# A float32 product split into three float32r products, in a fused convolution and feed-forward kernel

## The chip, the cores and the metric

The kernel runs on one core of a Trainium2 chip. The metric is the device time of one execution in microseconds (us). Three executions of the kernel before took 2501.99, 2504.36 and 2504.86 us; the median is 2504.36 us.

## The reference

Eight batches of 3008 positions x 256 channels are convolved along the positions by a filter given in the frequency domain. The result, 24064 tokens of 256 values, goes through a feed-forward layer whose activation is a rational function.

```python
X = np.fft.rfft(x, axis=1)                  # x: (8, 3008, 256), float32
y = np.fft.irfft(X * (filt_r + 1j * filt_i), n=3008, axis=1)
h = y.reshape(24064, 256) @ w_in            # w_in: (256, 2048)
P = a[0] + a[1] * h + a[2] * h**2 + a[3] * h**3
Q = 1.0 + abs(b[0]) * abs(h) + abs(b[1]) * h**2
out = (P / (Q + 1e-06)) @ w_out             # w_out: (2048, 256)
```

## The kernel before

The Fourier transform of length 3008 = 64 x 47 is done as matrix products in three stages. Stage 1 is the transform of length 47 (the matmuls `s`, L435), with sums and differences made by GpSimd beforehand (`fold`, L382). Stage 2 works on 128 rows x 512 columns at a time, twelve pieces `i` for each batch. `product` multiplies the piece by the forward 64-point matrix (`y`, L488: one float32 matmul, which the trace records as two). VectorE multiplies the result by the two filter tiles (L492, L493), and GpSimd makes the complex product of them: `cross` twice (L504, two operations each), then `total` (L510). `halves` splits the sum into two float32r parts, the upper one as a ScalarE copy (L516), the lower one as a GpSimd subtraction (L517). `inverse` multiplies by the inverse 64-point matrix, which is held in two parts as well, with three float32r matmuls (`z`, `product3`, L349), and VectorE copies the result out (L344). Stage 3 (`x`, L572) is the inverse transform of length 47. It gives tokens in chunks of five groups of 94, split into upper and lower parts by ScalarE (L581) and VectorE (L583).

The feed-forward layer runs in 752 units of 512 tokens x 128 hidden values. Each unit has six matmuls in (L606 to L609) and six out (L689 to L691), all float32r, 128 x 512. Between them ScalarE makes five passes, VectorE four (`p` L657, `g_hi` L666, `rest` L674, `g_lo` L680), each with one operand in PSUM, and GpSimd two (`pool_m` L671, `pool_q1` L652). The four passes of VectorE on one unit are spread over several units of program order: `product_out` of unit i - 4 is issued with `product_in` of unit i, after what the convolution puts between. In the last 128 units half of the squares move from ScalarE to GpSimd.

The order of work on TensorE, ScalarE, VectorE and GpSimd is written out by hand. The convolution of the next batch is a generator that the loop over units advances (`pipeline`, L886). Each item that it yields has a cost. A credit grows by 0.6 per unit for batch 1 and by 0.38 for the others, and one item at most is issued per unit. A bare `yield` puts what follows into the next unit:

```python
            if i > 0:
                yield from s.inverse(i - 1)
            if i < 12:
                s.cross(i, 0, 1)
                yield
                s.total(i)
                yield
                s.halves(i)
```

So a step (one y and one z) takes at least four units: y's, z's with the second `cross`, one with `total`, one with `halves`. A stage 3 chunk puts two units of its own in between when its time has come, in all for one chunk in 14 or 15 units. If a chunk needs a batch whose convolution isn't finished, the rest of that batch is issued at once, with no unit between (`run(gen or conv_items(nxt))`, L934).

Batch 0 is done in the head (`head`, L719), where `Plan` (L110) orders the steps by a list of durations and due times and gives each raw weight tile the home that comes free first. Weights 14 and 15 are loaded at unit 0 into fixed homes (`RAW`, L56): 15 into a home of "oe", the tag of the output tiles, of which there are two.

## Time and profile before

| | before |
|---|---|
| median of three executions | 2504.36 us |
| the profiled execution | 2504.63 us |
| its span, first to last instruction | 2502.8 us |
| mean granted share of TensorE's clock | 0.990 |
| TensorE busy | 2451.5 us, 98% |
| VectorE busy | 2279.7 us, 91% |
| ScalarE busy | 2340.8 us, 94% |
| GpSimd busy | 2103.9 us, 84% |

"Busy" is the time in which at least one instruction of the engine runs. Instructions of an engine overlap at their ends, so the time from one start to the next is what an instruction costs its engine, and it is a little shorter than its recorded duration: a 128 x 512 float32r matmul is recorded with 0.39 us, and the next one starts 0.227 us later. The head takes about the first 81 us. The seven further batches run beside the units up to about 2060 us. After that the units run alone.

In the views PE is TensorE, DVE VectorE, ACT ScalarE, POOL GpSimd and SP SyncE, whose queue issues the DMAs. L488 is line 488 of the kernel.

### The profile page before, as it was taken

How to read it: one execution, taken by the hardware profiler on the slowest of the kernel's cores; microseconds unless marked ns; L12 is line 12 of the kernel's file. 1: busy time of each engine (PE TensorE's matmuls, PEld its weight loads, DVE VectorE, ACT ScalarE, POOL GpSimd, SP SyncE). 2: the span in 40 equal slices, each digit the busy share in tenths (PEclk: the TensorE clock that was granted, in tenths of full speed). 3: DMA queues.
4: the chain of work that ended last, by engine and by line, in shares of the span. 5: the costliest groups of instructions: out<-in, count | busy, mean ns of one | idle time of the engine just before them, and what ended most of it. 6: DMA issues, size and time to landing. Idle time of an engine off the chain costs nothing.

```text
span 2502.8 us, 36529 instructions
## 1 busy us (share of the span) xinstructions
PE 2451.5 (98%) x10950; PEld 1958.0 (78%) x10950; DVE 2279.7 (91%) x3554; ACT 2340.8 (94%) x4139; POOL 2103.9 (84%) x2261
## 2 busy tenths in 40 slices
PE   7799989999999999999999999999999999999998
PEld 4578867878787877888788887887788788888887
DVE  7789978999889998999889998899889999999998
ACT  6699979999999999999999999999999999999997
POOL 7788987899868997889868998789868897888887
PEclk9799999999999999999999999999999999999999
DMA  7443242322323232332323322332322210100000
GB/s 264 142 111 89 85 115 77 112 82 84 98 78 100 85 92 78 91 105 84 90 84 90 93 86 77 96 100 84 95 86 81 62 42 17 33 17 17 25 10 19
DMA packets 98727, 205.12 MB, mean 82 GB/s; under 512 B 7967, under 2 KB 54559, under 8 KB 98519
## 3 DMA queue, kind: packets, MB, share of 16 engines
q1 hardware_dynamic: 98519, 202.70, 27.2%
q8 instruction: 88, 1.44, 0.3%
q14 instruction: 120, 0.98, 0.1%
HBM read 130.49 MB, written 72.17 MB: 81 GB/s over the span
## 4 chain that ended last, share of the span: by engine, by line
PE 85%; POOL 6%; DVE 5%; issue 2%; ACT 1%; DMA 1%; SPq 0%; POOLq 0%; DVEq 0%; ACTq 0%
PE o L689 12%; PE o L690 12%; PE o L691 12%; PE h_u L606 12%; PE h_u L607 12%; PE h_u L609 12%; PE x L572 4%; PE s L435 3%; PE y L488 3%; POOL q_u L671 2%; PE z L349 2%; POOL q_u L652 1%; DVE h_u L674 1%; DVE hi_u L666 1%; POOL a_u L640 1%
## 5 line engine op out<-in xcount | busy, mean ns | idle before, releaser
L671 POOL TENSOR_TENSOR q_u<-q_u,hi_u 128x512 f32<-128x512 f32 x752 | 975.3, 1297 | 253.5 <-DVE hi_u L666 231.4
L689 PE MATMUL o<-hi_u,wo_sb 128*128 128x512 f32 x1504 | 660.4, 439 | 0.0
L666 DVE SCALAR_TENSOR_TENSOR hi_u<-h_u,scal,a_u 128x512 fp32r<-128x512 f32 x752 | 557.4, 741 | 51.5 <-ACT a_u L642 44.6
L606 PE MATMUL h_u<-xhl,wi_sb 128*128 128x512 f32 x1504 | 593.5, 395 | 3.9 <-DVE raw L313 3.8
L690 PE MATMUL o<-lo_u,wo_sb 128*128 128x512 f32 x1504 | 588.3, 391 | 7.7 <-DVE lo_u L680 7.7
L691 PE MATMUL o<-hi_u,wo_sb 128*128 128x512 f32 x1504 | 588.5, 391 | 0.0
L607 PE MATMUL h_u<-xhl,wi_sb 128*128 128x512 f32 x1504 | 587.9, 391 | 0.0
L674 DVE SCALAR_TENSOR_TENSOR h_u<-h_u,scal,q_u 128x512 f32<-128x512 f32 x752 | 563.7, 750 | 25.4 <-POOL q_u L671 24.5
L657 DVE SCALAR_TENSOR_TENSOR h_u<-w_u,scal,h_u 128x512 f32<-128x512 f32 x752 | 560.2, 745 | 5.2 <-ACT w_u L621 5.2
L632 ACT ACTIVATE a_u<-q_u,scal 128x512 f32<-128x512 f32 x752 | 549.2, 730 | 0.0
L627 ACT ACTIVATE q_u<-q_u,scal 128x512 f32<-128x512 f32 x752 | 546.8, 727 | 1.9
L652 POOL TENSOR_SCALAR q_u<-q_u,scal 128x512 f32<-128x512 f32 x752 | 526.8, 700 | 1.5 <-ACT a_u L632 1.4
L621 ACT ACTIVATE w_u<-h_u,scal 128x512 f32<-128x512 f32 x752 | 519.6, 691 | 0.0
L614 ACT ACTIVATE q_u<-h_u 128x512 f32<-128x512 f32 x752 | 454.3, 604 | 65.3 <-PE h_u L609 52.2
L680 DVE TENSOR_TENSOR lo_u<-h_u,a_u 128x512 fp32r<-128x512 f32 x752 | 512.5, 682 | 0.1
L609 PE MATMUL h_u<-xhl,wi_sb 128*128 128x512 f32 x1504 | 465.3, 391 | 0.0
L642 ACT ACTIVATE a_u<-a_u 128x512 f32<-128x512 f32 x688 | 438.4, 637 | 0.0
L690 PEld LDWEIGHTS o<-lo_u,wo_sb 128*128 128x128 f32 x1504 | 283.5, 188 | 98.6 <-issue 37.5
L689 PEld LDWEIGHTS o<-hi_u,wo_sb 128*128 128x128 f32 x1504 | 283.3, 188 | 89.2 <-issue 35.7
L606 PEld LDWEIGHTS h_u<-xhl,wi_sb 128*128 128x128 f32 x1504 | 283.7, 189 | 70.0 <-DVE lo_u L680 5.2
L607 PEld LDWEIGHTS h_u<-xhl,wi_sb 128*128 128x128 f32 x1504 | 283.7, 189 | 60.9 <-issue 1.4
L691 PEld LDWEIGHTS o<-hi_u,wo_sb 128*128 128x128 f32 x1504 | 282.7, 188 | 61.2
(93 smaller groups left out, 2250.2 us busy)
## 6 DMA issues: line engine op xcount, KB each, us to landing
f<-filt SPq DMA_DIRECT2D x168, 256.0 KB, 3.8
xin<-xp SPq DMA_DIRECT2D x48, 512.0 KB, 3.5
scr<-ev SPq DMA_DIRECT2D x48, 512.0 KB, 2.8
outT<-oe SPq DMA_DIRECT2D x47, 512.0 KB, 2.7
tl<-scr SPq DMA_DIRECT2D x45, 480.0 KB, 4.0
xin<-scr SPq DMA_DIRECT2D x42, 512.0 KB, 4.7
scr<-xin SPq DMA_DIRECT2D x42, 480.0 KB, 3.3
raw<-w_in SPq DMA_DIRECT2D x8, 512.0 KB, 8.2
```

The source lines that it names most:

```text
L606: nc.tensor.matmul(o, w_in_part(0, f, cc), xh[:, cc, ts], start=cc == 0, stop=False)
L607: nc.tensor.matmul(o, w_in_part(0, f, cc), xl[:, cc, ts], start=False, stop=False)
L609: nc.tensor.matmul(o, w_in_part(1, f, cc), xh[:, cc, ts], start=False, stop=cc == 1)
L632: nc.scalar.activation(self.a, self.q, AF.Abs_reciprocal_sqrt, bias=QK)
L652: nc.gpsimd.tensor_scalar(out=self.q, in0=self.q, scalar1=1.0, scalar2=QK, op0=ALU.mult, op1=ALU.add)
L657: v.scalar_tensor_tensor(out=H, in0=w, scalar=PK, in1=H, op0=ALU.add, op1=ALU.mult)
L666: nc.vector.scalar_tensor_tensor(out=self.hi, in0=self.H, scalar=self.p0, in1=self.a, op0=ALU.add, op1=ALU.mult)
L671: nc.gpsimd.tensor_tensor(out=self.q, in0=self.q, in1=self.hi.bitcast(F32), op=ALU.mult)
L674: nc.vector.scalar_tensor_tensor(out=self.H, in0=self.H, scalar=self.p0, in1=self.q, op0=ALU.add, op1=ALU.subtract)
L689: nc.tensor.matmul(o, w_out_part(0, f, dd), self.hi, start=f == 0, stop=False)
L690: nc.tensor.matmul(o, w_out_part(0, f, dd), self.lo, start=False, stop=False)
L691: nc.tensor.matmul(o, w_out_part(1, f, dd), self.hi, start=False, stop=f == 15)
```

## The change

The forward matrix `fwd_sb` is held in two float32r parts (upper and lower half, made in `mats_upper` and `mats_lower` by one more GpSimd subtraction). For batches 1 to 7 the input of `product` is split as well: `split` copies the piece to float32r on ScalarE, `split_lower` subtracts on VectorE, and `product` uses `product3`. Piece i + 1 is split while step i is in its z unit and the unit after. In batch 1 (`b > 1` is false) the bare `yield` between `cross` and `total` is left out. The parts live in a new tile "yr" with one buffer, and the output tile "oe" goes from two buffers to one to make room. In the head "yr" serves as a home for one input tile and for weights in the place of the second "oe". The scalars move to a smaller tile with other columns.

```diff
-    fwd_sb = consts.tile([128, 128], F32, name="fwd_sb")
+    fwd_sb = consts.tile([128, 2, 128], F32R, name="fwd_sb")
...
-            nc.tensor.matmul(yt, fwd_sb, self.flat(self.tin[q], j), start=True, stop=True)
+            product3(yt, fwd_sb, *self.y.pop(i))
...
+        def split(self, i):
+            q, j = divmod(i, 2)
+            y = self.flat(self.tin[q], j)
+            tile = conv.tile([128, 2, TT], F32R, tag="yr", name=f"yr{self.b}_{i}", bufs=1)
+            hi, lo = self.y[i] = tile[:, 0], tile[:, 1]
+            nc.scalar.activation(hi, y, AF.Copy)
+
+        def split_lower(self, i):
+            q, j = divmod(i, 2)
+            hi, lo = self.y[i]
+            v.tensor_tensor(out=lo, in0=self.flat(self.tin[q], j), in1=hi.bitcast(F32), op=ALU.subtract)
...
         for i in range(13):
+            if i == 0:
+                s.split(0)
+                s.split_lower(0)
             if i < 12:
                 yield from s.product(i)
             if i > 0:
                 yield from s.inverse(i - 1)
             if i < 12:
                 s.cross(i, 0, 1)
-                yield
+                if i < 11:
+                    s.split(i + 1)
+                if b > 1:
+                    yield
                 s.total(i)
+                if i < 11:
+                    s.split_lower(i + 1)
                 yield
                 s.halves(i)
...
-        ev = conv.tile([128, 2, T], F32, tag="oe", name=f"oe{t}")
+        ev = conv.tile([128, 2, T], F32, tag="oe", name=f"oe{t}", bufs=1)
...
-        plan = Plan(8 - T * 2 // TT, dict(xin=XB, oe=2, tl=2, ev=2, f1=FB, f2=FB, raw=1))
+        plan = Plan(8 - T * 2 // TT, dict(xin=XB, oe=1, yr=1, tl=2, ev=2, f1=FB, f2=FB, raw=1))
...
-            n, tag = width(t), ("xin", "xin", "xin", "xin", "oe", "oe", "tl")[t]
+            n, tag = width(t), ("xin", "xin", "xin", "xin", "oe", "yr", "tl")[t]
...
-            for out, of, rows in ((inv_sb, pair[0], slice(0, 64)), (inv_sb, pair[1], slice(64, 128))):
+            for out, of, rows in ((fwd_sb, pair[3], slice(0, 128)), (inv_sb, pair[0], slice(0, 64)), (inv_sb, pair[1], slice(64, 128))):
                 nc.gpsimd.tensor_tensor(out=out[rows, 1], in0=of[rows], in1=out[rows, 0].bitcast(F32), op=ALU.subtract)
...
-ring=(("raw", "oe", "xin") + (("tl",) if k < 7 else ()), f"{n}whole"), pick=w)
+ring=(("raw", "oe", "yr", "xin") + (("tl",) if k < 7 else ()), f"{n}whole"), pick=w)
```

## Rows read from the trace of the kernel before

**Rows 1.** Windows, batch 3's stage 2: us, busy by engine (count), clock, DMA share, GB/s.

```profile
core 0: us, PE busy (x) PEld busy (x) DVE busy (x) ACT busy (x) POOL busy (x), PEclk, DMA share, GB/s
737.10:915.50 178.40, 178.20 (x798) 143.24 (x797) 170.42 (x268) 169.28 (x302) 158.97 (x180) 1.00 0.28 83
```

**Rows 2.** Timeline of TensorE in one step of batch 2's stage 2.

```profile
start us, us, engine line op out<-in xcount [idle before <-releaser]
...
566.41 0.39 PE L606 MATMUL h_u<-xhl,wi_sb 128*128 128x512 f32 x1
...
567.77 1.02 PE L488 MATMUL y<-xin,fwd_sb 128*128 128x512 f32 x2
...
570.03 0.39 PE L606 MATMUL h_u<-xhl,wi_sb 128*128 128x512 f32 x1
...
573.44 0.39 PE L606 MATMUL h_u<-xhl,wi_sb 128*128 128x512 f32 x1
...
576.16 0.39 PE L606 MATMUL h_u<-xhl,wi_sb 128*128 128x512 f32 x1
...
577.75 0.39 PE L690 MATMUL o<-lo_u,wo_sb 128*128 128x512 f32 x1
```

**Rows 3.** Timeline of GpSimd in the same step and the next.

```profile
559.77 0.69 POOL L652 TENSOR_SCALAR q_u<-q_u,scal 128x512 f32<-128x512 f32 x1
...
572.37 0.70 POOL L652 TENSOR_SCALAR q_u<-q_u,scal 128x512 f32<-128x512 f32 x1
...
574.19 1.30 POOL L671 TENSOR_TENSOR q_u<-q_u,hi_u 128x512 f32<-128x512 f32 x1
575.48 0.70 POOL L652 TENSOR_SCALAR q_u<-q_u,scal 128x512 f32<-128x512 f32 x1
576.15 1.29 POOL L510 TENSOR_TENSOR f<-f,zw 128x512 f32<-128x512 f32 x1
```

**Rows 4.** Timeline of VectorE, the same stretch.

```profile
572.61 0.68 DVE L344 COPY ev<-z 128x512 f32<-128x512 f32 x1
573.21 0.75 DVE L674 SCALAR_TENSOR_TENSOR h_u<-h_u,scal,q_u 128x512 f32<-128x512 f32 x1
...
574.52 0.68 DVE L680 TENSOR_TENSOR lo_u<-h_u,a_u 128x512 fp32r<-128x512 f32 x1
...
575.78 0.75 DVE L674 SCALAR_TENSOR_TENSOR h_u<-h_u,scal,q_u 128x512 f32<-128x512 f32 x1
...
578.75 0.76 DVE L674 SCALAR_TENSOR_TENSOR h_u<-h_u,scal,q_u 128x512 f32<-128x512 f32 x1 [0.31 <-POOL q_u L671]
```

**Rows 5.** Timeline of TensorE at the end of batch 1's stage 2.

```profile
333.36 0.50 PE L349 MATMUL z<-zr,inv_sb 128*128 128x512 f32 x1 [1.75 <-POOL zr L517]
...
337.44 2.14 PE L349 MATMUL z<-zr,inv_sb 128*128 128x512 f32 x3 [2.72 <-ACT zr L516]
342.86 2.15 PE L349 MATMUL z<-zr,inv_sb 128*128 128x512 f32 x3 [3.27 <-ACT zr L516]
```

**Rows 6.** Timelines of GpSimd and VectorE in the head.

```profile
7.30 0.21 POOL L227 TENSOR_SCALAR scal<-small_sb 128x1 f32<-128x1 f32 x1
7.53 2.58 DVE L382 TENSOR_TENSOR xs<-xin 120x512 f32<-120x512 f32 x4 [1.30 <-DMA xin<-xp]
7.59 0.67 POOL L228 TENSOR_TENSOR scal<-scal 128x1 f32<-128x1 f32 x1
...
50.37 0.41 DVE L301 TENSOR_SCALAR wp<-wt 128x512 uint32<-128x512 uint32 x1
...
61.21 1.59 DVE L301 TENSOR_SCALAR wp<-wt 128x512 uint32<-128x512 uint32 x1
61.23 1.28 POOL L318 TENSOR_TENSOR wt<-wt,raw 128x512 f32<-128x512 f32 x1
```

**Rows 7.** Timeline of SyncE's queue ahead of batch 3's stage 2; the page's DMA issues.

```profile
726.82 2.04 SPq L479 DMA_DIRECT2D xin<-scr  x4
...
xin<-scr SPq DMA_DIRECT2D x42, 512.0 KB, 4.7
```

**Rows 8.** Timelines of GpSimd and TensorE at the end of the head.

```profile
82.26 1.30 POOL L318 TENSOR_TENSOR wt<-wt,raw 128x512 f32<-128x512 f32 x1
...
88.29 1.25 PE L572 MATMUL x<-small_sb,tl 96*128 96x96 f32 x10
```

More of the change, by code (lines that the diff above doesn't have):

```diff
@@ L49 @@
 XB, FB = 4, 3
+HOMES = {"raw": {"bufs": 1}, "oe": {"bufs": 1}, "yr": {"bufs": 1}, "xin": {"bufs": XB}, "f1": {"bufs": FB}, "f2": {"bufs": FB}}
 FIRST = (0, 1, 4, 5, 2, 3, 8, 9, 6, 7, 12, 13, 10, 11)
@@ L178, in conv_moe @@
     mlp = ctx.enter_context(tc.tile_pool(name="mlp", bufs=1))
+    last = ctx.enter_context(tc.tile_pool(name="last", bufs=1))
     ps = ctx.enter_context(tc.tile_pool(name="ps", bufs=1, space=PSUM))
@@ L190, in conv_moe @@
     e_sb = small_sb[:R1, 2 * R0 : 2 * R0 + GE]
-    scal = consts.tile([128, 64], F32, name="scal")
-    ab_sb, abs_sb, cf_sb = small_sb[:, AB : AB + 12], scal[:, 12:24], scal[:, 24:40]
-    flag_sb = scal[:, 40:41].bitcast(I32)
+    scal = last.tile([128, 32], F32, name="scal")
+    ab_sb, abs_sb, cf_sb = small_sb[:, AB : AB + 12], scal[:, :12], scal[:, 12:28]
+    flag_sb = scal[:, 28:29].bitcast(I32)
     v = nc.vector
@@ L254, in load @@
             tag = self.tag
-            bufs = {"raw": 1, "xin": XB, "f1": FB, "f2": FB}.get(tag)
+            bufs = HOMES.get(tag, {})
             if tag == "tl":
@@ L258, in load @@
             else:
-                raw = conv.tile([128, TT, 2], U32, tag=tag, name=f"raw{i}", **({"bufs": bufs} if bufs else {}))
+                raw = conv.tile([128, TT, 2], U32, tag=tag, name=f"raw{i}", **bufs)
             self.l, self.h = raw[:, :, 0], raw[:, :, 1]
@@ L445, in __init__ @@
         def __init__(self, b):
-            self.b, self.f, self.tin, self.ev, self.z, self.sides, self.parts = b, {}, {}, {}, {}, {}, {}
+            self.b, self.f, self.tin, self.ev, self.z, self.sides, self.parts, self.y = b, {}, {}, {}, {}, {}, {}, {}
         def tl(self, tag, q, **kw):
@@ L729, in x_load @@
             else:
-                tile = conv.tile([128, 2, n], F32, tag=tag, name=f"xin0_{t}", **({"bufs": XB} if tag == "xin" else {}))
+                tile = conv.tile([128, 2, n], F32, tag=tag, name=f"xin0_{t}", **HOMES.get(tag, {}))
             first[t] = stage1_load(0, t, tile)
@@ L741, in mats_upper @@
         def mats_upper():
-            for out, of, rows in ((inv_sb, pair[0], slice(0, 64)), (inv_sb, pair[1], slice(64, 128))):
+            for out, of, rows in ((fwd_sb, pair[3], slice(0, 128)), (inv_sb, pair[0], slice(0, 64)), (inv_sb, pair[1], slice(64, 128))):
                 nc.scalar.activation(out[rows, 0], of[rows], AF.Copy)
-            nc.scalar.activation(fwd_sb, pair[3], AF.Copy)
         def mats_lower():
-            for out, of, rows in ((inv_sb, pair[0], slice(0, 64)), (inv_sb, pair[1], slice(64, 128))):
+            for out, of, rows in ((fwd_sb, pair[3], slice(0, 128)), (inv_sb, pair[0], slice(0, 64)), (inv_sb, pair[1], slice(64, 128))):
                 nc.gpsimd.tensor_tensor(out=out[rows, 1], in0=of[rows], in1=out[rows, 0].bitcast(F32), op=ALU.subtract)
@@ L815, in head @@
         v.memset(still, 1.0)
-        nc.scalar.activation(scal[:, 48:49], still[:, :1], AF.Abs_reciprocal_sqrt)
+        nc.scalar.activation(scal[:, 29:30], still[:, :1], AF.Abs_reciprocal_sqrt)
         for _ in range(3):
@@ L822, in head @@
         for t in range(7):
-            add(f"x{t}", lambda t=t: x_load(t), "SP", 0.5, due=-20 + t, moves=1.4 if t < 6 else 0.7, ring=(("xin", "xin", "xin", "xin", "oe", "oe", "tl")[t], f"sum{min(2 * t + 1, 12)}"))
+            add(f"x{t}", lambda t=t: x_load(t), "SP", 0.5, due=-20 + t, moves=1.4 if t < 6 else 0.7, ring=(("xin", "xin", "xin", "xin", "oe", "yr", "tl")[t], f"sum{min(2 * t + 1, 12)}"))
             if t == 0:
@@ L853, in head @@
             eased = i in EASED
-            add(f"{n}load", w.load, "SP", 0.5, due=8 + 2.8 * k if k < 6 else 25 + 5 * (k - 6), moves=1.4, ring=(("raw", "oe", "xin") + (("tl",) if k < 7 else ()), f"{n}whole"), pick=w)
+            add(f"{n}load", w.load, "SP", 0.5, due=8 + 2.8 * k if k < 6 else 25 + 5 * (k - 6), moves=1.4, ring=(("raw", "oe", "yr", "xin") + (("tl",) if k < 7 else ()), f"{n}whole"), pick=w)
             add(f"{n}mag", w.magnitude, "ACT", 0.53, [f"{n}load"] + ([f"w{FIRST[k - 1]}shift"] if k else []), due=late, bank=f"{n}power" if eased else f"{n}rest", filler=True)
```

## Prediction

> **What bounds the kernel now.** I read the windows of one batch's stage 2 first, then each engine's timeline in one step of it, then TensorE's timeline around the end of batch 1, and last the weight phase, where a behaviour of VectorE beside GpSimd shows. The window of batch 3's stage 2 [rows 1] is to be read engine by engine: TensorE is busy for 178.20 of 178.40 us at the full granted clock, VectorE for 170.42, ScalarE for 169.28, GpSimd for 158.97. So TensorE sets the pace, and the others have 8 to 19 us of air in 178. The reader should keep both facts: a microsecond taken from TensorE counts only while no other engine becomes later than it, and they stand close behind.
>
> How close is seen in one step. Most steps of stage 2 take four units. On TensorE a plain unit lasts 573.44 to 576.16, that is 2.72; the unit with a y product 566.41 to 570.03, that is 3.62; the one with a z product 570.03 to 573.44, that is 3.41 [rows 2]. So y costs 0.90, z 0.69, and a four-unit step 4 x 2.72 + 0.90 + 0.69 = 12.47. GpSimd's same step runs from 559.77 to 572.37, that is 12.60 without a gap [rows 3]: it is over TensorE's pace already, and only the longer steps between, which hold a stage 3 pair, let it catch up. VectorE's plain unit is 573.21 to 575.78, that is 2.57, and a copy of 512 columns 572.61 to 573.21, that is 0.60 [rows 4]; four units with the two y products and the copy of z, three operations of that size, make 12.08, and some 0.17 for its part of an output tile (one such operation in 16 units). Its idle 0.31 ahead of a "rest" is a wait for GpSimd [rows 4]. Between VectorE and TensorE there is a reserve: the lower half that ends at 574.52 + 0.68 = 575.20 [rows 4] is read by the matmul at 577.75 [rows 2], 2.55 later.
>
> **Part 1, the product y.** One float32 product (two matmul records) becomes three float32r matmuls of the form that z already has, with the same columns and the same two-part weights. Per product 0.90 - 0.69 = 0.21; 84 products (12 in each of 7 batches): -17.6 us of TensorE time. Both prices stand in neighbouring units, so this term has little doubt; what it is worth hangs on the engines behind.
>
> **Part 2, the forced end of batch 1.** Counting the program's slots by its own rule (credit 0.6 a unit, one item a slot), batch 1's stage 2 begins at unit 30 and is at its tenth product when chunk 7 calls for it at unit 73; what is left is emitted in one piece with no unit between. That is seen on TensorE as idle times of 1.75, 2.72 and 3.27 ahead of z matmuls, and the last two triples last 2.14 and 2.15 [rows 5], some 1.3 more than a triple's 0.69 and the tail of its last record. Idle 7.74, the two slow triples 2 x 1.3, and an estimated 1.6 for what else runs at that pace around them: 12 us in all. With one emission step less, a step of batch 1 takes three units, and the same count ends at unit 70. The order is fixed when the program is built, so the forced pass is surely gone: -12. But three units are only 3 x 2.72 + 2 x 0.69 = 9.54 on TensorE, and GpSimd has for them what it has for four less one plain unit of 1.29 + 0.67 = 1.96 [rows 3]: 12.60 - 1.96 = 10.64. Here GpSimd becomes the bound, whatever part 3 costs.
>
> **Part 3, the split.** It adds per product one copy on ScalarE and one subtraction on VectorE, 84 of each. The copy is not dearer than VectorE's of the same size, 0.60 [rows 4]: ScalarE's 169.28 [rows 1] plus 12 x 0.60 is 176.5, about what TensorE's 178.40 - 12 x 0.21 = 175.9 leaves. I cost it at nothing of its own; if this cover is gone it is 0.6 a batch, and all 7.2 if ScalarE's air lies elsewhere. VectorE's price is 0.60 by the copy's row, but this operation differs from the others of the stage: both its inputs lie in SBUF, while each of the others reads PSUM on one side. Nothing in the trace shows such an operation beside a large one of GpSimd, so it is bounded from neighbours [rows 6]. From below: 0.60, and nothing for GpSimd. It can't be below that, since nothing is taken from VectorE for it. From above: the SBUF to SBUF operation of the weight phase takes 0.41 alone and 1.59 when a GpSimd operation of 1.28 starts with it, so up to 1.18 more on VectorE. And the small operations of GpSimd take 0.21 before VectorE's additions of two SBUF inputs (the group at 7.53) and 0.67 beside them, ending when the addition ends. I take the two as one thing: GpSimd stands still for the 0.60 of each subtraction, and VectorE waits for what GpSimd has in flight. In the step shown the subtraction would come where "rest" now starts, at 575.78 [rows 4], while GpSimd is in the operation that ends when the next begins at 576.15 [rows 3]: 0.37, of which 0.31 is idle anyway.
>
> The Trainium skill, page "SBUF — State Buffer", section "Who interferes with whom", says this of the shared port: a VectorE instruction with two SBUF inputs contends with a GpSimd instruction that reads SBUF, and the second to issue blocks until the first is finished. It speaks against putting the lower half on VectorE. Of its two sides the trace shows one on small operations, GpSimd's 0.67 for 0.21. By it alone each subtraction could cost up to 0.60 + 1.28 on VectorE; without it the sum below would be some 8 us lower.
>
> So a four-unit step needs 12.60 + 0.60 = 13.20 on GpSimd and 12.25 + 0.60 to 0.97 = 12.85 to 13.22 on VectorE, against 12.47 - 0.21 = 12.26 on TensorE. Two or three such steps follow each other; then comes one of six units with a stage 3 pair, in which GpSimd wins back all (two plain units are 3.9 for it and 5.4 plus the pair for TensorE) and VectorE some 0.8. A run of three adds 2.8 of lag on GpSimd, and 1.8 to 2.8 on VectorE to what VectorE kept from the run before; the reserve of 2.55 swallows the first of it. By this tally what shows on TensorE in a batch of 12 steps is about 1.2 us: 6 x 1.2 = +7.2 for batches 2 to 7. Ends: 0, and, if nothing were absorbed, 8 x 0.94 = 7.5 a batch, +45.
>
> In batch 1 a three-unit step needs 10.64 + 0.60 = 11.24 on GpSimd against 9.54: +1.7 in each of nine steps. The two-unit first step adds 3, and the two five-unit steps with a stage 3 pair give back 1.9 each: 3 + 9 x 1.7 - 3.8 = 14.5, less the reserve at the end, some 2: +12.5. Ends: +5 (no lock, three-unit steps at 1.1 over) and +15. Chunk 7 now finds batch 1 finished three units before its load; z's eviction, store and load back are a chain about as long as what TensorE does meanwhile, and VectorE is late there: +1.5 (0 to 3).
>
> **Smaller moves.** The first split of a batch waits on ScalarE for a load, with ScalarE's whole unit behind it. That load is issued at 726.82, after the last store, and takes 4.7 [rows 7]; the first product comes at 737.1 (the window's start), so the copy, a unit earlier, finds the data: nothing, and if the load were 3 us late, up to 3 a batch. The output tile has one buffer for two: it is filled once in 16 units, some 44 us, so the wait is nothing. In the head the plan gives the same order on every queue, and the same homes except that weight 9 goes to "yr". But weight 15's load then takes the one "oe" home, held by weight 11 until GpSimd's operation at 82.26 ends at 83.56 [rows 8]; the load of chunk 2, queued behind it on SyncE, can then go out at about 84, and its product is at 88.29 [rows 8], 4.3 later, against 4.7 for a load of like size [rows 7]: +0.5 (0 to 3). One more small subtraction on GpSimd and the renamed scalars cost nothing that shows.
>
> **Sum.** The profiled execution took 2504.6 us (span 2502.8, 1.8 around it), 0.3 from the median of 2504.4. 2504.6 - 17.6 - 12 + 12.5 + 1.5 + 7.2 + 0.5 = 2496.7; I predict 2497.
>
> **Rivals.** A, no contention: the subtraction costs 0.60 on VectorE and nothing elsewhere. Batch 1 then loses 6 and the other batches about 1 each: 2504.6 - 17.6 - 12 + 6 + 1 + 6 + 0.5 = 2488.5. For it: no row shows this very pair of operations; against it: GpSimd's 0.67 for 0.21 [rows 6].
>
> B, slower: the lock between VectorE and GpSimd becomes the pace of stage 2. Its place is the run of four-unit steps, its price 0.94 a step over TensorE, and it decides once the reserve isn't there at the start of each run, because the stage 3 step leaves VectorE late instead of even. With two thirds of the 7.5 showing in each batch, 6 x 5 = 30 stand for 7.2, and batch 1 at +15 for 12.5: 2496.7 + 22.8 + 2.5 = 2522. For it: GpSimd has no gap in such a step and VectorE already waits for it [rows 3, 4]; against it: 8 us of VectorE's air in the batch [rows 1]. From about a third of the price on, the kernel is slower than now.
>
> C, no difference: the reserve is half used up. Then 3 a batch show, 18 for 7.2: 2507. That the change doesn't do what it says, three passes as dear as the float32 product, is nearly excluded by z's 0.69.
>
> **How the numbers follow.** Forecast (2490 to 2500) 0.42, A (below 2490) 0.13, C (2500 to 2510) 0.23, B 0.22. What a measurement of this kernel can tell from no change is about 0.2%, 5 us either way of 2504.4: faster is below 2499.4, A and nearly all of the forecast, 0.54; same is C and the edge, 0.24; slower is B, 0.22. The range goes from A's lower end, 2482, to 2518, where three quarters of the slow side lie inside or at its edge.
>
> **What would show it.** Right: a y unit at 3.41; no idle of over 1 us before z in batch 1, and TensorE stalls there that name GpSimd's or VectorE's results; batches 3, 5 and 7 at 176 to 178 us from first to last product where they took 178.4; the subtraction at 0.7 to 1.9, longest beside a GpSimd operation. Wrong: the subtraction always at 0.68 and GpSimd's durations unchanged (A), or stage 2 at over 180 us a batch (B). A forced pass still in batch 1, or a first copy of a batch that stands on its load, would overturn parts 2 and 3.

## The result and the profile after

The change made the kernel slower: 2535.03 us median of four executions (2531.05 to 2536.87) against 2503.18 for the kernel before beside it, a ratio of 1.0124 [1.0111, 1.0137]. The prediction was 2497, with a range of 2482 to 2518. The profiled execution of after took 2531.05 us (span 2529.2), the lowest of the four, and the one of before 2504.6, 1.4 over its median; so the two traces differ by 26.4 us where the medians differ by 31.9.

**Busy time and chain of the page.** First the line of busy times, then the chain that ended last.

```profile
PE 2452.9 (97%) x11034; PEld 1964.4 (78%) x11034; DVE 2338.8 (92%) x3638; ACT 2379.4 (94%) x4223; POOL 2138.2 (85%) x2262
...
PE 50%; DVE 19%; POOL 15%; ACT 8%; issue 6%; DMA 1%; DVEq 0%; POOLq 0%; SPq 0%; ACTq 0%
```

TensorE's busy time is what it was (2451.5). In the chain of before TensorE held 85%, GpSimd 6 and VectorE 5; now TensorE holds half, and VectorE and GpSimd a third.

**Windows**, from the first y product to the last z product: batches 3 and 4 after, and below them batch 4 before; columns as in [rows 1].

```profile
743.95:925.43 181.48, 178.20 (x810) 144.98 (x809) 180.84 (x283) 174.64 (x314) 163.89 (x181) 1.00 0.27 81
1031.99:1207.75 175.76, 171.80 (x768) 138.21 (x766) 174.73 (x273) 168.77 (x303) 159.70 (x176) 1.00 0.28 82
...
1022.06:1192.86 170.80, 170.44 (x755) 136.57 (x754) 163.90 (x258) 162.31 (x290) 154.76 (x176) 1.00 0.29 85
```

Against [rows 1] batch 3 takes 181.48 for 178.40, and batch 4 takes 175.76 for 170.80. In batch 3 TensorE was idle for 0.2 us and is now for 3.3; VectorE goes from 170.42 to 180.84, 0.6 short of the whole window.

**One four-unit step** of batch 2, TensorE, VectorE, GpSimd; it answers to [rows 2 to 4].

```profile
start us, us, engine line op out<-in xcount [idle before <-releaser]
578.48 0.39 PE L628 MATMUL h_u<-xhl,wi_sb 128*128 128x512 f32 x1
...
581.20 0.39 PE L628 MATMUL h_u<-xhl,wi_sb 128*128 128x512 f32 x1
...
582.56 0.84 PE L351 MATMUL y<-yr,fwd_sb 128*128 128x512 f32 x3
583.24 0.39 PE L711 MATMUL o<-hi_u,wo_sb 128*128 128x512 f32 x1
...
584.73 0.50 PE L628 MATMUL h_u<-xhl,wi_sb 128*128 128x512 f32 x1
...
586.68 0.94 PE L351 MATMUL z<-zr,inv_sb 128*128 128x512 f32 x3 [0.29 <-DVE f L495]
...
571.54 0.73 DVE L688 SCALAR_TENSOR_TENSOR hi_u<-h_u,scal,a_u 128x512 fp32r<-128x512 f32 x1
...
579.14 1.04 DVE L520 TENSOR_TENSOR yr<-xin,yr 128x512 fp32r<-128x512 f32 x1
580.11 0.75 DVE L696 SCALAR_TENSOR_TENSOR h_u<-h_u,scal,q_u 128x512 f32<-128x512 f32 x1
...
584.60 0.73 DVE L688 SCALAR_TENSOR_TENSOR hi_u<-h_u,scal,a_u 128x512 fp32r<-128x512 f32 x1
...
572.75 0.69 POOL L674 TENSOR_SCALAR q_u<-q_u,scal 128x512 f32<-128x512 f32 x1
...
578.96 0.69 POOL L674 TENSOR_SCALAR q_u<-q_u,scal 128x512 f32<-128x512 f32 x1
579.62 1.72 POOL L524 TENSOR_TENSOR f<-f,zw 128x512 f32<-128x512 f32 x1
581.29 1.30 POOL L693 TENSOR_TENSOR q_u<-q_u,hi_u 128x512 f32<-128x512 f32 x1
...
585.78 0.69 POOL L674 TENSOR_SCALAR q_u<-q_u,scal 128x512 f32<-128x512 f32 x1
```

The y triple now has z's shape: the next matmul after 582.56 starts at 583.24, 0.68 later, where it took 0.90. The subtraction (L520) takes VectorE from 579.14 to 580.11, 0.97 instead of 0.60, and the `total` that GpSimd starts inside it at 579.62 takes 1.72 instead of the 1.29 of [rows 3]. VectorE's step is 584.60 - 571.54 = 13.06, GpSimd's 585.78 - 572.75 = 13.03; TensorE's own work, by the prediction's prices, is 12.26.

**Waits**: two of before, then those of after (engine, line, what it waited for: us in total, times, longest).

```profile
ACT q_u L614 <- PE h_u L609: 52.2, 82, 2.4
...
PEld h_u L606 <- DVE lo_u L680: 5.2, 13, 0.6
```

```profile
PEld h_u L628 <- DVE lo_u L702: 37.9, 54, 2.2
ACT zr L530 <- POOL f L524: 36.3, 49, 1.8
...
ACT q_u L636 <- PE h_u L631: 27.8, 42, 2.1
...
PE h_u L628 <- DVE lo_u L702: 18.4, 38, 1.7
...
DVE yr L520 <- ACT yr L515: 13.2, 7, 2.0
```

The weight load (PEld) ahead of `product_in` waited 13 times for `g_lo`; now 54 times, seven times as long in all, and the matmul itself 38 times. `g_lo` is the operation that gives a unit's PSUM bank back, so it is the bank that the new unit waits for. ScalarE's wait for TensorE has halved: TensorE no longer leads. In batches 2 to 7 alone TensorE's matmuls stand idle for 11.4 us before `product_in` on `g_lo` (none before), for 4.0 before z on the second filter product (0.8 before) and for 3.8 before y on the stage 3 subtraction (0.9 before). All three are operations of VectorE. The last line, seven waits of about 1.9, one in each batch, comes back below.

**Where the time went.** The first `product_in` matmul of a unit marks its start. From a batch's start to the next one's is one number per batch; for batch 3, units 193 and 281, first before, then after:

```profile
735.77 0.39 PE L606 MATMUL h_u<-xhl,wi_sb 128*128 128x512 f32 x1
...
1020.72 0.39 PE L606 MATMUL h_u<-xhl,wi_sb 128*128 128x512 f32 x1
```

```profile
742.62 0.39 PE L628 MATMUL h_u<-xhl,wi_sb 128*128 128x512 f32 x1
...
1030.64 0.39 PE L628 MATMUL h_u<-xhl,wi_sb 128*128 128x512 f32 x1
```

That is 284.95 and 288.02: +3.1. The table does this for each kernel that was run, as differences to the kernel before, in us; "batch 1" is units 31 to 105, "even" the mean of batches 2, 4 and 6 (from units 105, 281 and 457), "odd" that of 3, 5 and 7 (from 193, 369 and 545 to 640), and the sum is over all six. The ratios are of the whole time, with their 95% interval; the kernel before took 2501.9 to 2503.2 us (median) beside these kernels. Units 640 to 751 agree to 0.05 in all. The weight phase and the first 31 units scatter by up to 2.7 from one profile to the next, also where nothing is changed there, and are left out.

| kernel | ratio | batch 1 | even | odd | sum 2 to 7 |
|---|---|---|---|---|---|
| after | 1.0124 [1.0111, 1.0137] | +3.3 | +5.1 | +3.1 | +24.5 |
| e1_parts_once | 0.9996 [0.9986, 1.0006] | -1.9 | +0.3 | -0.8 | -1.5 |
| e2_copies_only | 1.0001 [0.9992, 1.0011] | 0.0 | +0.4 | -0.7 | -1.0 |
| e3_one_sbuf_input | 1.0024 [1.0014, 1.0035] | -0.4 | +1.8 | +0.6 | +7.3 |
| e4_two_sbuf_inputs_there | 1.0122 [1.0105, 1.0139] | +4.8 | +5.0 | +3.1 | +24.1 |
| e5_yield_alone | 0.9995 [0.9985, 1.0004] | -2.7 | 0.0 | 0.0 | -0.1 |
| e6_split_alone | 1.0120 [1.0102, 1.0138] | +5.2 | +4.7 | +3.0 | +22.9 |
| e7_lower_on_gpsimd | 1.0307 [1.0290, 1.0324] | +10.4 | +11.8 | +9.8 | +64.5 |
| e8_parts_once_no_zlow | 0.9964 [0.9951, 0.9977] | -9.3 | -0.2 | -0.8 | -3.1 |
| e9_before_no_zlow | 0.9977 [0.9966, 0.9988] | -4.7 | -0.3 | 0.0 | -1.0 |
| e10_changed_no_zlow | 1.0046 [1.0029, 1.0063] | -2.0 | +2.6 | +1.2 | +11.6 |
| e11_first_pair_apart | 1.0089 [1.0073, 1.0106] | +0.9 | +2.8 | +3.6 | +19.2 |
| e12_parts_once_apart | 0.9981 [0.9972, 0.9991] | -4.8 | -1.4 | -0.2 | -4.7 |
| e13_apart_z_copy_on_act | 0.9992 [0.9982, 1.0002] | -4.8 | -0.6 | +0.1 | -1.6 |
| e14_before_z_copy_on_act | 1.0003 [0.9994, 1.0013] | -0.9 | +0.1 | 0.0 | +0.3 |
| e15_apart_no_zlow | 0.9939 [0.9923, 0.9956] | -9.7 | -2.0 | -0.5 | -7.6 |
| e16_apart_both_lighter | 0.9940 [0.9924, 0.9957] | -9.8 | -1.9 | -0.4 | -6.9 |
| e17_apart_not_moved | 0.9968 [0.9957, 0.9978] | -1.6 | -1.4 | -1.9 | -10.0 |
| e18_before_moved | 1.0019 [1.0009, 1.0029] | +1.8 | -0.4 | +1.0 | +1.7 |

Batch 1 as a whole came out at +3.3; the miss lies in batches 2 to 7, where the prediction had -15.1 for y and +7.2 for the lag, -7.9, and the trace has +24.5.

### The profile page after: what moved, and what is told of

Read it like the earlier page. It is cut to its first block, busy times and chain, and to the rows that moved or that the text cites. A ratio compares the mean times of both kernels' runs of the same rounds, so it can differ in the third digit from the quotient of the medians.

```text
span 2529.2 us, 36885 instructions
## 1 busy us (share of the span) xinstructions
PE 2452.9 (97%) x11034; PEld 1964.4 (78%) x11034; DVE 2338.8 (92%) x3638; ACT 2379.4 (94%) x4223; POOL 2138.2 (85%) x2262
## 4 chain that ended last, share of the span: by engine, by line
PE 50%; DVE 19%; POOL 15%; ACT 8%; issue 6%; DMA 1%; DVEq 0%; POOLq 0%; SPq 0%; ACTq 0%
PE o L711 7%; PE o L712 7%; PE o L713 7%; PE h_u L628 7%; PE h_u L629 7%; PE h_u L631 7%; POOL q_u L693 5%; DVE hi_u L688 5%; DVE h_u L696 4%; DVE h_u L679 3%; PE s L437 3%; POOL f L524 3%; PE x L594 3%; POOL zw L506 3%; POOL q_u L674 2%
## 5 line engine op out<-in xcount | busy, mean ns | idle before, releaser
L711 PE MATMUL o<-hi_u,wo_sb 128*128 128x512 f32 x1504 | 627.2, 417 | 0.0
L713 PE MATMUL o<-hi_u,wo_sb 128*128 128x512 f32 x1504 | 587.1, 390 | 0.0
L696 DVE SCALAR_TENSOR_TENSOR h_u<-h_u,scal,q_u 128x512 f32<-128x512 f32 x752 | 562.4, 748 | 19.4 <-POOL q_u L693 18.8
L636 ACT ACTIVATE q_u<-h_u 128x512 f32<-128x512 f32 x752 | 454.5, 604 | 31.9 <-PE h_u L631 27.8
```

The costliest lines, as they stand in the source:

```text
L696: nc.vector.scalar_tensor_tensor(out=self.H, in0=self.H, scalar=self.p0, in1=self.q, op0=ALU.add, op1=ALU.subtract)
L711: nc.tensor.matmul(o, w_out_part(0, f, dd), self.hi, start=f == 0, stop=False)
L713: nc.tensor.matmul(o, w_out_part(1, f, dd), self.hi, start=False, stop=f == 15)
```

## The experiments

**What the split costs, built up in four kernels.** In e1 no split is made after piece 0: its two parts stand for all twelve pieces of a batch (so the convolution of batches 1 to 7 is not that of the reference). e2 adds ScalarE's copy for every piece, without the subtraction. e2 to e4 give another output as well, since most of their lower halves are not those of the piece. e3 adds a VectorE operation of the same size right behind z's copy for ten pieces of a batch, with z's PSUM bank as its second input; the first two pieces are split as in after. e4 is its control at the same place, with both inputs in SBUF (y minus y).

```diff
 e1, against after
+                s.first = s.y[0]
 ...
-                    s.split(i + 1)
+                    s.y[i + 1] = s.first
 ...
-                if i < 11:
-                    s.split_lower(i + 1)
 e2, against after (and one yr tile for a batch)
-                if i < 11:
-                    s.split_lower(i + 1)
 e3, against after, in inverse() behind z's copy (e4: in1=y)
+            if i + 2 < 12:
+                self.split(i + 2)
+                y = self.flat(self.tin[(i + 2) // 2], (i + 2) % 2)
+                v.tensor_tensor(out=self.y[i + 2][1], in0=y, in1=zt, op=ALU.subtract)
 ...
-                if i < 11:
+                if i == 0:
                     s.split(i + 1)
 ...
-                if i < 11:
+                if i == 0:
                     s.split_lower(i + 1)
```

> The changed kernel, but the parts of a batch's first piece stand for all twelve, so eleven of twelve copies on ScalarE and subtractions on VectorE are left out of each batch (the output is another). TensorE does the same. If the loss comes from the split at all, what remains is the gain: 2503 - 17.6 - 12, and some 5 to 8 lost in batch 1's three-unit steps to GpSimd: 2479 to 2483. If the loss comes from elsewhere (the products themselves, the one output buffer, the head's homes), the time stays over 2520.

> The changed kernel with every copy on ScalarE, but the subtraction on VectorE for the first piece of a batch alone (the others' lower half is left out, the output is another). If VectorE's subtraction is the cause, the copies cost nothing and the time is that of the kernel without a split, within 4 us. If ScalarE, which had 9 us of air in a batch of 178, is the bound, some 0.5 a step shows, 40 us over it.

> The changed kernel with VectorE's operation right behind z's copy out, and its second input read from z's PSUM bank in place of SBUF (the output is another; same size, same engine). Shared access to SBUF as the cause of the step's 13.05: it falls to 12.85, VectorE's operation to 0.68 recorded, GpSimd's total from 1.60 to 1.30, and the time by 48 x 0.2 in batches 2 to 7 and some 4 in batch 1, to about 2520. VectorE's own 0.60 as the whole cause: no change from the changed kernel, 2530 to 2536. Shared access as the whole cause: about 2485.

> The control of the run before: the operation at the same place, both inputs from SBUF (the piece itself twice, so without the wait for ScalarE's copy; the output is another). Shared access: VectorE's operation at 0.8 to 1.1 recorded, a GpSimd operation beside it 0.3 to 0.5 longer, 2530 to 2536, some 12 over the run before. No shared access: the same time as the run before.

Measured: 2502.08, 2503.23, 2509.32 and 2533.33 us. Three things follow. ScalarE's copies cost nothing (e1 to e2). VectorE's 0.60 costs 8 us by itself in batches 2 to 7 (-1.0 to +7.3), and sharing SBUF with GpSimd another 17 there and 24 in all (e3 to e4). e3 came out 11 us below the 2520 expected of it, so sharing costs twice the 12 us that had been put on it. And e1 missed its expectation: with no split after piece 0 the kernel is no faster than before. Two questions were left, where TensorE's gain of 17.6 and the 12 of the forced pass went, and on whom the lock falls.

On whom it falls is in the groups of e3 and e4 (busy us, mean ns) and in one stretch of e4:

```profile
L545 DVE TENSOR_TENSOR yr<-xin,z 128x512 fp32r<-128x512 f32 x70 | 47.2, 674 | 0.0
...
L506 POOL TENSOR_SCALAR zw<-f,sgn_sb 64x256 f32<-64x256 f32 x336 | 157.4, 477 | 89.7 <-issue 41.4 <-DVE f L494 35.6 <-POOL q_u L678 2.7
```

```profile
L545 DVE TENSOR_TENSOR yr<-xin 128x512 fp32r<-128x512 f32 x70 | 51.3, 733 | 0.0
...
L506 POOL TENSOR_SCALAR zw<-f,sgn_sb 64x256 f32<-64x256 f32 x336 | 187.9, 568 | 85.3 <-issue 40.0 <-DVE f L494 32.6
```

```profile
783.60 0.68 DVE L545 TENSOR_TENSOR yr<-xin 128x512 fp32r<-128x512 f32 x1
784.20 0.76 DVE L700 SCALAR_TENSOR_TENSOR h_u<-h_u,scal,q_u 128x512 f32<-128x512 f32 x1
...
780.53 0.93 POOL L506 TENSOR_SCALAR zw<-f,sgn_sb 64x256 f32<-64x256 f32 x2
...
783.62 1.47 POOL L506 TENSOR_SCALAR zw<-f,sgn_sb 64x256 f32<-64x256 f32 x2
```

In e4 the subtraction starts 0.02 ahead of a `cross` pair of GpSimd and keeps its 0.60; the pair takes 1.47 for 0.93. In after it starts while GpSimd is in `pool_q1`, waits, and then holds up `total`. In both stretches the operation that comes second pays, and both places cost the kernel the same: 1.0122 and 1.0124.

**The two parts of the change alone.** e5 is the kernel before with only batch 1's emission step taken out; e6 is after with it put back.

```diff
 e5, against before
-                yield
+                if b > 1:
+                    yield
 e6, against after
-                if b > 1:
-                    yield
+                yield
```

> The kernel before with batch 1's emission step taken out and nothing else (y stays a float32 product, no split). Theory (GpSimd is the pace of batch 1 in three-unit steps, so the forced pass is only spread over the units ahead of it): 2502, that is 2499 to 2506; units 31 to 74 take longer and 74 to 105 shorter by about the same. Prediction's part 2 (the forced pass is worth 12 us, three-unit steps cost 5 of them): 2497 or below.

> The changed kernel with batch 1's emission step put back: only the y product and its split. Theory (batches 2 to 7 cost 24.5 us by the starts of their units, and batch 1 pays some 3 to 6 for the same subtraction in front of its forced pass): 2530 to 2534. Rival (the dropped emission step is itself a large part of the loss, since GpSimd is pressed there): below 2526. Rival (the dropped step did save its 12 us, hidden under the lock): 2540 or above.

Measured: 2501.67 and 2533.75, both as the theory said. So the step left out is worth next to nothing (batch 1 -2.7 in the profile, 0.9995 in time), and the loss is the split's. The starts of the units show why: in e5 units 31 to 73 take 14.1 us longer than before, and from unit 73 to 105, with the forced pass gone, 16.9 less.

**Who ate the gain: GpSimd lighter.** In e8 (on e1) and e9 (on before) z's lower half is subtracted for piece 0 of each batch alone and stands for the other eleven, which takes 1.25 per step off GpSimd; e10 is the same on after.

```diff
-            tile = conv.tile([128, 2, TT], F32R, tag="raw", name=f"zr{self.b}_{i}", bufs=1)
+            if i == 0:
+                self.parts_z = conv.tile([128, 2, TT], F32R, tag="raw", name=f"zr{self.b}_{i}", bufs=1)
+            tile = self.parts_z
 ...
-            nc.gpsimd.tensor_tensor(out=lo, in0=z, in1=hi.bitcast(F32), op=ALU.subtract)
+            if i == 0:
+                nc.gpsimd.tensor_tensor(out=lo, in0=z, in1=hi.bitcast(F32), op=ALU.subtract)
```

> The kernel with y's parts of piece 0 reused, and z's lower half too written for piece 0 alone: GpSimd has one subtraction of 1.25 less in each step, TensorE the same work. Theory (GpSimd, at 12.60 against TensorE's 12.26, hid TensorE's gain): the gain shows now, 2.5 us in each of batches 2 to 7 and 5 to 15 in batch 1: 2477, that is 2468 to 2484, a batch's stage 2 at 174.5 and 182 where it was 177.2 and 184. Rival (the three float32r passes save TensorE nothing in the run of units, whatever the records say): 2498 to 2503, batches 2 to 7 as before.

> The kernel before with z's lower half written for piece 0 of each batch alone: GpSimd has one subtraction of 1.25 less in each step, TensorE the same work as before. Theory (in the kernel before TensorE is the pace of batches 2 to 7, GpSimd close behind): batches 2 to 7 within 0.7 us of before each; batch 1's forced pass, a chain through GpSimd, some 3 to 8 shorter: 2497, that is 2493 to 2502. Rival (GpSimd was the pace already): 1 us or more less in each batch, 2492 or below.

> The changed kernel with z's lower half written for piece 0 of each batch alone, so that GpSimd has 1.25 less in each step. Theory (the lock costs because VectorE itself, at 4 x 2.57 + 3 x 0.60 + 0.97 = 13.05 a step, is over TensorE's 12.26): batches 2 to 7 within 1 us of the changed kernel, batch 1 some 8 shorter: 2527, that is 2522 to 2531. Rival (GpSimd, held up by 0.44 a step, is what is late): batches 2 to 7 back near the kernel before, 2502 to 2510.

Measured: 2494.07, 2497.61 and 2513.95. In batch 1 the theory held: e8 is 7.4 shorter there than e1 (-9.3 and -1.9), so GpSimd was the pace of the three-unit steps. In batches 2 to 7 it fell: e8 gains 1.6 over e1 in all six together, not 15. GpSimd did not hide TensorE's gain there. e9 came out as expected: batch 1 is 4.7 shorter and the others are within 0.5. In e10 neither side was right: the six batches go from +24.5 to +11.6. That is not GpSimd's lag alone, since with fewer GpSimd operations the subtraction itself waits less, 774 ns on average for 917. How much of the loss under the lock is GpSimd's and how much VectorE's is thus not shown. VectorE is still busy for all but 0.9 of batch 3 (the window's row):

```profile
738.78:918.43 179.65, 177.33 (x811) 145.24 (x809) 178.72 (x283) 174.43 (x314) 152.35 (x170) 1.00 0.29 82
```

**The subtraction on GpSimd.** e7 keeps the whole change and moves y's lower half to GpSimd.

```diff
-            v.tensor_tensor(out=lo, in0=self.flat(self.tin[q], j), in1=hi.bitcast(F32), op=ALU.subtract)
+            nc.gpsimd.tensor_tensor(out=lo, in0=self.flat(self.tin[q], j), in1=hi.bitcast(F32), op=ALU.subtract)
```

> The changed kernel with y's lower half subtracted on GpSimd: VectorE as before, no two engines on the same SBUF operands. Theory (GpSimd has no gap in a four-unit step, so 12.60 + 1.25 = 13.85 against TensorE's 12.26, and the longer steps win only part of it back): slower than the changed kernel, 2550, that is 2538 to 2565. Rival (GpSimd's idle time in the longer steps takes it up): 2505 to 2520.

Measured: 2578.42, beyond the expected range on the slow side. The group is `L520 POOL`, 84 of 1302 ns; by the price of 13.85 a step GpSimd is the late engine, and a batch takes 10 to 12 us longer. What a six-unit step gives back was overrated here too.

**The start of a batch.** The profile of e1 still had the seven waits of VectorE for ScalarE's copy. In after, batch 4's first split is this, on VectorE and ScalarE:

```profile
1028.95 0.74 DVE L688 SCALAR_TENSOR_TENSOR hi_u<-h_u,scal,a_u 128x512 fp32r<-128x512 f32 x1
1031.53 0.82 DVE L520 TENSOR_TENSOR yr<-xin,yr 128x512 fp32r<-128x512 f32 x1 [1.84 <-ACT yr L515]
...
1030.83 0.67 ACT L515 ACTIVATE yr<-xin 128x512 fp32r<-128x512 f32 x1
```

Copy and subtraction are issued in one unit. ScalarE runs behind VectorE in the unit, takes the copy in its place, and VectorE stands 1.84 us in front of it, with the next `rest`, `p` and `g_lo` queued behind and TensorE's next bank behind `g_lo`. e11 (on after) and e12 (on e1) put a unit between the two:

```diff
                 s.split(0)
+                yield
                 s.split_lower(0)
```

> The changed kernel with one unit between the first copy of a batch (ScalarE) and its subtraction (VectorE). Theory (at each batch's start VectorE stands 1.84 us for that copy, and nothing gives it back: some 2 us in each of 7 batches): 2522, that is 2518 to 2526. Rival (in the longer step with a stage 3 pair the stall is won back, or hidden under the lag of the subtractions): 2532 to 2537.

> The same unit of distance in the kernel with y's parts of piece 0 reused. Theory (the stall at the batch's start is what ate TensorE's 2.5 us a batch there, since units 296 to 333 show 3.40 for 3.62 at each y product): 2489, that is 2486 to 2493; a batch's stage 2 some 2 us shorter than 177.2 and 183.8, the extra unit counted out. Rival (another engine at its limit takes the place of TensorE): 2499 to 2503.

Measured: 2525.48 and 2497.67. e11's time is in its range: against the kernel before beside each, the loss goes from 31.9 to 23.1 us. But the gain was to be some 2 us in every batch, and it isn't: batch 1 and the even batches are 2.4 and 2.3 shorter than in after, the odd ones 0.5 longer. e12 missed, with half of what it should have gained: even batches -1.4, odd ones -0.2.

**What holds the odd batches.** Four kernels made VectorE lighter, GpSimd lighter, and both, the first of them beside a control. In e13, e14 and e16 z's copy out of PSUM goes to ScalarE; e15 and e16 leave z's lower half at piece 0; e13, e15 and e16 stand on e12.

```diff
 e13, e14, e16
-EV1, EV2, EVO = "A", "V", "AV"
+EV1, EV2, EVO = "A", "A", "AV"
```

> y's parts of piece 0 reused, the first pair apart, and z's copy out of PSUM moved from VectorE to ScalarE: VectorE has 0.60 less in each step. Theory (behind TensorE it is VectorE that is late, since its lower half gives the PSUM bank back to the next unit): the rest of TensorE's gain shows, 2488, that is 2484 to 2492; even batches at about 174.5, odd ones at 182.5. Rival (GpSimd is what is late): 2496 to 2500.

> The kernel before with z's copy out of PSUM moved from VectorE to ScalarE, as the control. Theory (TensorE is the pace of batches 2 to 7 there, but VectorE's lag shows in the steps with a stage 3 pair): each batch 0 to 1 shorter, 2499, that is 2496 to 2504. Rival (VectorE was as much the pace as TensorE): below 2493. ScalarE too full for it: above 2506.

> y's parts of piece 0 reused, the first pair apart, and z's lower half written for piece 0 of each batch alone: GpSimd has 1.25 less in each step. Theory (VectorE is what is late): batch 1 some 8 shorter as before, batches 2 to 7 within 0.7 us of those without it: 2489, that is 2486 to 2492. Rival (GpSimd): batches 2 to 7 at 174.5 and 182, 2478 or below.

> All three: parts of piece 0, first pair apart, z's copy on ScalarE, z's lower half for piece 0 alone. With VectorE and GpSimd both lighter, TensorE's gain must show whole if it is one: batches 2 to 7 at 174.4 and 182.0, batch 1 shorter too: 2478, that is 2473 to 2484. If the batches stay over 176 and 184, the three passes save less in the run of units than the records of one unit say.

Measured: 2499.97, 2503.38, 2487.79 and 2487.47; e13 and e16 missed, e14 and e15 are in their ranges. With 0.60 less on VectorE in each step e13 gains nothing over e12 (-1.6 against -4.7). That doesn't clear VectorE, since the copy now lies on ScalarE. GpSimd was hardly it: e15 is 0.6 and 0.3 shorter per batch than e12, and half of its 10 us come from batch 1. With both lighter the even batches show -1.9 of TensorE's 2.5, and the odd ones still only -0.4. So the unit that e12 to e16 put in was tried next, since it moves every product. e17 is e12 with one empty unit fewer ahead of stage 2, so that all products have the units they have in e1; e18 is the kernel before with one more, and nothing else.

```diff
 e17 (e18: GAP + 1)
-        for _ in range(GAP):
+        for _ in range(GAP - 1):
```

> y's parts of piece 0 reused, one unit between the first copy and its subtraction, and one empty unit fewer ahead of it, so that the products keep their units. Theory (the stall at the start is the loss, and the moved unit is what kept the odd batches from showing it): even batches about 175.5, odd ones about 182.3, in all 2491, that is 2487 to 2495. Rival (the odd batches lose to an engine): odd ones at 183.7 or more, 2497 or above.

> The kernel before with one more empty unit ahead of each stage 2, nothing else: every product comes one unit later. Theory (a product that falls into a unit where an output tile waits costs some 1 us; two such in the odd batches, one in the even): odd batches 1 to 2 longer, even ones 0 to 1 longer, 2509, that is 2505 to 2513. Rival (the place of the products is worth nothing): 2501 to 2504.

Measured: 2494.42 and 2506.42, both in the theory's range. The price of the moved unit is the difference of e12 and e17, in which the products of batches 3 to 7 lie one unit apart (the first of an odd batch three): 1.8 us in an odd batch, nothing in an even one. e18 moves more than its expectation says. Its y products start one unit later than before in most of batch 2, and two or four later in batches 3 to 7: +1.0 in an odd batch, as expected, and -0.4 in an even one, where 0 to 1 more had been expected. So the place of the products counts; that a waiting output tile is the reason was not tested by itself. e17 takes 8.6 us off batches 2 to 7 of e1 (-10.0 and -1.5) by removing the stall alone, and its odd batches gain 1.9 each. On VectorE and ScalarE the start of batch 4 in e17 reads:

```profile
1014.61 0.68 DVE L520 TENSOR_TENSOR yr<-xin,yr 128x512 fp32r<-128x512 f32 x1
...
1012.73 0.66 ACT L515 ACTIVATE yr<-xin 128x512 fp32r<-128x512 f32 x1
```

Of TensorE's 2.5 a batch the odd ones of e17 thus still miss 0.6. That sits behind the stage 3 pairs. From the starts of units 212 to 214 (y, z, none) the kernel before takes 3.62 + 2.27 + 4.21 = 10.10, and e17 3.40 + 2.49 + 4.22 = 10.11; at units 244 to 246 it is 9.99 and 10.00, and at unit 198 5.46 and 5.47. Elsewhere a y unit falls from 3.62 to 3.40 and nothing gives it back. So three y products of twelve lie where TensorE waits for something else. The trace of e17 says what: on TensorE, the y of unit 198 and the start of unit 214.

```profile
749.38 0.97 PE L351 MATMUL y<-yr,fwd_sb 128*128 128x512 f32 x3 [0.26 <-DVE xhl L605]
...
799.88 0.50 PE L628 MATMUL h_u<-xhl,wi_sb 128*128 128x512 f32 x1 [0.29 <-DVE lo_u L702]
```

Both wait for VectorE, the first for its stage 3 subtraction, the second for `g_lo`, and unit 246 waits 0.16 for `g_lo` as well. In the even batches of e17, 1.1 are missing; of that, two z units at the start of batch 4 (units 285 and 289) hold 0.64, 3.76 and 3.82 for 3.44 and 3.50. By the program's own rule for banks z takes the bank that y had there, and z starts some 0.15 after VectorE's second filter product, which gives it back. So most of what is missing of TensorE's gain is lost where VectorE hands a bank over late; that is read from the trace, and no run tests it.

No kernel with the whole computation was measurably faster than the one before. The split with the stall removed and the products not moved was not run.

## Why the prediction was wrong

**Part 1, y from 0.90 to 0.69: the price was right, the place was not looked at.** The triple takes 0.68. With eleven of twelve splits left out and without the stall e17 shows 10.0 of the 15.1 us of batches 2 to 7. The missing third lies mostly behind the stage 3 pairs and at the starts of the even batches, where TensorE waits for VectorE. The prediction said that a microsecond counts only while no other engine becomes later, and then counted TensorE's whole gain, on its 178.20 of 178.40 [rows 1]; in those steps it does not count.

**Part 2, the forced end of batch 1: gone as counted, and worth far less.** In after the last z products of batch 1, now in their own units, read on TensorE:

```profile
329.90 0.94 PE L351 MATMUL z<-zr,inv_sb 128*128 128x512 f32 x3 [0.27 <-ACT w_u L643]
...
335.99 0.73 PE L351 MATMUL z<-zr,inv_sb 128*128 128x512 f32 x2 [1.05 <-ACT zr L530]
338.49 0.50 PE L351 MATMUL z<-zr,inv_sb 128*128 128x512 f32 x1 [1.77 <-POOL zr L531]
```

They answer to [rows 5]: idle times of 0.27, 1.05 and 1.77 stand for 1.75, 2.72 and 3.27, so "no idle of over 1 us" was not quite met. That GpSimd becomes the bound was said, and e8 shows it. But the lower end put on it, 5 us without a lock, was too low. In e5 the units from 73 on win 16.9 and the ones before lose 14.1. Of both, an estimated 3.9 is only the two y and three z products that unit 73 held and that now come earlier (0.90 and 0.69 each). So the forced pass was worth 13, and three-unit steps alone cost 10. With the lock, and with the stall of the first split, the terms of batch 1 come to 3.3 + 2.5 + 13 = 18.8, where 12.5 + 1.5 had been put. Batch 1 ended 4 us above its forecast of -0.5: the cost was missed by 5, and a gain 1 larger than forecast hid part of it.

**Part 3, the split: the four-unit step was counted right, the absorption of its lag was wrong.** The absorption is the step of the prediction that failed. The prediction gave GpSimd 13.20 and VectorE 12.85 to 13.22 in a four-unit step; measured are 13.03 and 13.06. It gave VectorE a wait of 0.37; the subtraction takes 0.97 for 0.60. Then it let "the reserve of 2.55" and the six-unit steps swallow the lag, so that 1.2 a batch would show, 7.2 in all, with 45 as the upper end. Measured, from e2 to e4: 25.1, of which 8.2 are VectorE's own 0.60 and 16.8 the lock. The reserve had been read at the wrong hand-over. It was taken from the lower half to the matmul that reads it (L680 to L690), but the same operation also gives its PSUM bank to a later `product_in`. In the trace of before, first a unit behind a z unit, then unit 214, with the weight load that stood ahead of it:

```profile
770.34 0.68 DVE L680 TENSOR_TENSOR lo_u<-h_u,a_u 128x512 fp32r<-128x512 f32 x1
...
772.43 0.39 PE L606 MATMUL h_u<-xhl,wi_sb 128*128 128x512 f32 x1
...
803.22 0.68 DVE L680 TENSOR_TENSOR lo_u<-h_u,a_u 128x512 fp32r<-128x512 f32 x1
...
803.96 0.50 PE L606 MATMUL h_u<-xhl,wi_sb 128*128 128x512 f32 x1
...
803.96 0.19 PEld L606 LDWEIGHTS h_u<-xhl,wi_sb 128*128 128x128 f32 x1 [0.48 <-DVE lo_u L680]
```

The bank of the first is free at 771.02 and taken at 772.43: a reserve of 1.41, not 2.55. The second is free at 803.90 and taken at 803.96: none at all. Unit 214 comes three units behind a stage 3 pair (210 and 211), which the prediction had win back the lag. The unit ahead of it has no `product_out`: the program (L954) holds the first one of each output tile back, so TensorE asks for the next bank six matmuls, 1.36 us, sooner. Of the 13 such waits in before, 12 lie at this place, the second unit after an output tile's last `product_out`. So there TensorE already waited for VectorE, and no lag could be absorbed. In after, batch 3 reads like this in an ordinary step too:

```profile
847.36 0.68 DVE L702 TENSOR_TENSOR lo_u<-h_u,a_u 128x512 fp32r<-128x512 f32 x1
...
848.09 0.50 PE L628 MATMUL h_u<-xhl,wi_sb 128*128 128x512 f32 x1
```

Bank free at 848.04, matmul at 848.09. That is rival B in the main: the reserve isn't there behind a stage 3 pair, though B did not see that the output tile's end takes it. B's price is nearly right as well: it let two thirds of the full 7.5 a batch show, and 25.1 of 45 is 56%. B's sign, a stage 2 of over 180 us, is met in batch 3 with 181.48.

**The first split of a batch: nothing expected, 8.6 measured.** The prediction asked whether the data would be there for ScalarE's copy, and they were. It did not ask who waits for the copy. The subtraction was issued in the same unit, and VectorE takes its operations in the order written: it stands some 1.9 us in each batch, with its unit behind it. Removing the stall takes the six batches from -1.5 to -10.0 (e1 to e17).

**Where nothing was expected and nothing came:** ScalarE's copies (e2), the single output tile (units 640 to 751 unchanged).

**The half microsecond in the head: right in kind.** In after the load of chunk 2 goes out at 84.64, where about 84 had been forecast, and its product on TensorE waits for it:

```profile
89.78 1.35 PE L594 MATMUL x<-small_sb,tl 96*128 96x96 f32 x10 [0.79 <-DMA tl<-scr]
```

The unit with it (2) is 1.0 us longer than before. In the whole time it can't be told, since unit 0 itself starts 0.7 earlier to 1.5 later from one profile to the next.

**Sum for batches 2 to 7:** -10.0 (y where it counts) + 8.6 (stall at the start, e17 to e1) + 0.5 (copies, e1 to e2) + 8.2 (the subtraction, e2 to e3) + 16.8 (lock, e3 to e4) + 0.4 (its place, e4 to after) = +24.5. The terms are differences along one order of kernels, and another order would share them out differently: in e11 the stall's removal, with every product moved by a unit, gives back 5.4 of the 8.6.

## What to carry to other kernels

Before a microsecond of the busiest engine is counted as a gain, or a lag as absorbed, look for the tightest hand-over from the engine behind it, the return of a buffer as well as the data, and look in every kind of step; one step with no reserve ends the credit. Where two engines' operations are issued in the same slot and one reads the other's result, ask which of the engines runs behind in that slot: the other one stands there, with all that is queued behind. And an operation with both inputs in SBUF on VectorE is to be priced with what GpSimd does at that moment on either side: the one that came second paid here.

## What the hardware showed that was not expected

The lock between VectorE and GpSimd is now seen on large operations, where before [rows 6] showed it on small operations of GpSimd and on a VectorE operation with one input. At 579.14 VectorE's subtraction starts beside a GpSimd operation with 0.5 us to go and takes 0.97 for 0.60; the GpSimd operation issued inside it takes 1.72 for 1.29. With the subtraction first (e4, 783.60) it keeps its 0.60 and GpSimd's pair goes from 0.93 to 1.47. With one input in PSUM (e3) neither grows: 674 and 477 ns on average, against 733 and 568 in e4. This is what the Trainium skill, page "SBUF — State Buffer", section "Who interferes with whom", says of the shared port, that the second to issue blocks until the first is finished, and that a VectorE operation with one SBUF input, outside its two-port modes, does not contend. The trace agrees with both, with waits somewhat shorter than a whole block: 0.37 where 0.51 of the first operation was left. In this full pipeline such pairs cost 24 us of 2533 for the 70 operations in which e3 and e4 differ, 0.34 each.

A recorded busy share hides the reserve: TensorE at 178.20 of 178.40 us looked like a bound without exception, and an engine at 170 of 178 like one with 8 us of air. At unit 214 the hand-over between them had 0.06 us.
